# The last batch's Gram products moved behind the third mixing, its softmax and mixing beside twelve early expert units

## The chip, the cores and the metric

The kernel runs on one core of a Trainium2 chip. The metric is the device time of one execution in microseconds (us), lower is better. A core has engines that each work through their own queue in order and wait for one another by semaphores: TensorE (PE, matmuls, with a weight load "PEld" ahead of each), VectorE (DVE), ScalarE (ACT), GpSimd (POOL, here only the issuer of indirect DMAs) and SyncE (SP, the issuer of plain DMAs). A matmul writes to PSUM, and ACT or DVE copies it out from there.

## The reference

Four batches of column-normalised channel attention, followed by a mixture of eight experts with one expert for each token:

```python
B, N, C = (4, 5056, 256)                 # q, k, v; in all 20224 tokens
qn = q / (np.linalg.norm(q, axis=1, keepdims=True) + 1e-06)
kn = k / (np.linalg.norm(k, axis=1, keepdims=True) + 1e-06)
s = kn.transpose(0, 2, 1) @ qn / tau
s = s - s.max(-1, keepdims=True)
a = np.exp(s)
a /= a.sum(-1, keepdims=True) + 1e-09
x = (v @ a)                              # 256 x 256 per batch, then N x 256

logits = x @ w_gate                      # E = 8 experts, hidden width 1024
e_idx = np.argmax(logits, axis=1)
gate_w = softmax(logits)[rows, e_idx]
eom = 1.0 / (1.0 + np.exp(-(x @ w_output_gate)))
h = np.maximum(x[mask] @ w1[e], 0.0)     # for each expert e, its tokens
out[mask] = gate_w[mask, None] * eom[mask, e, None] * (h @ w2[e])
```

## The kernel before

**Attention.** `gram(b)` reads q and k of a batch in 20 steps of 256 rows (tile `qk`, six buffers, loaded by SP). A step squares q and k on ACT (`sq`, L396), adds the squares on DVE (`acc`, L397), and adds eight matmuls (L409) to the 256 x 256 product in `s_ps`. After the 20 steps come twelve stages of the softmax: the copy `s_sb` (L418), the norms `k_ps` (L425), their spread over the columns `n_ps` (L447), the exponential (L458), the transposes `at_ps` (L467), the gate columns `aw_ps` (L477), and the split of the result into a high and a low part, `ah` and `al` (L489, L490). Pauses (`yield`) stand between the stages so that other work can be put beside them.

`mix(b)` needs `ah` and `al` of its batch. It has 20 steps of 256 tokens in five groups of four. A step turns v on PE (`turn`: `vt_ps` L519, cast `vh` L523 on ACT, rest `vl` L525 on DVE), does twelve matmuls into `x_ps` (L549 to L551), and copies them to `st` on ACT (L552). Three stages follow the 20 steps. At the end of a group, `route` finds the expert of each of its 1024 tokens with some fifteen small DVE rows and a few on ACT. Two steps later it counts the tokens of each expert with nine small matmuls (`r_ps`, L611 and L614), works out slots from the running counts `rco` (L619 to L624), and POOL scatters the group's rows to regions by expert in DRAM (`xs_d`, L627), in eight indirect DMAs.

**Experts.** `blocks` works in units of 256 (later some of 128) tokens of one expert: `fetch_x` reads their rows (`xg`; by SP for the units below 20, L894), `prepare` scales and splits them (`b_id` L913, `b_mx` L916, some small DVE rows, `xr` L946 on ACT and L947 on DVE, two transposing DMAs `xt` L951), `h_part` does four parts of twelve matmuls (`h_ps`, L972 to L974, copied out at L976 and L977), `y_part` four parts of twelve (`y_ps`, L996 to L998, copied out to `yo` at L1002), and `store` scatters the result by two indirect DMAs on POOL (L1009). A unit's y parts run beside the next unit's h parts; one `yield` of `blocks` is one such pair of parts, 24 matmuls. `x_ps`, `h_ps` and `r_ps` share four PSUM buffers; `vt_ps` and `y_ps` share three.

**Early units.** The place of a unit's rows depends on the counts. `checkpoint(False)` ranks the experts by their counts so far (`rank_experts`), has POOL read back a word of `xs_d` behind the scatters (`mark`, L640), from which it is known that they have landed, and fills the table of slots `gi` for the first units: L824 for the units of the fullest expert, L753 for the others. Here ten units run from it (`EARLY`), of which seven (`FIRST[1]`) are surely of the fullest expert. `checkpoint(True)` does the same for all others after the last mixing.

**Weights.** `prep_first` and `prep` bring an expert's weights (`raw`, 1 MB for each half), find the scale (L328 on ACT), split them into two 16-bit parts (L349 on ACT, L350 on DVE) and store these to DRAM (`wsc`, L358). `fetch_w` on POOL gathers them for a unit (L865). The fullest expert's weights stay in `wbuf`, and no fetch is needed for its units. `raw` of the later experts uses the four buffers of `st`.

**Order.** The bottom of the kernel writes the order out by hand: `_beside(main, (gen, rate))` takes `rate` steps of `gen` for each step of `main`. Gram 0 runs alone; its softmax beside the first steps of gram 1; mixings 0 to 2 beside the grams that are left, 1.3 steps for each of mixing; then `checkpoint(False)`, and the fourth mixing with no gram beside it, with the fullest expert's weights and from its twelfth step the first units. From this order a planner, which has its own idea of what each instruction costs, makes the queue of every engine: an instruction that is ready in its simulation may go ahead of one that is not. `main(...)` notes an instruction, and `behind` or `in_turn` tie others to places behind it on the same engine.

## Time and profile before

| | us |
|---|---|
| runs | 1291.0 (median of 3), 1288.16 to 1294.69 |
| the profiled execution | 1285.2, its span 1283.4 |
| PE busy in the span | 1201.1 (94%) |
| DVE, ACT, POOL busy | 702.2, 620.3, 572.5 |
| first matmul of a unit | at 374.67 |

The numbers of the profile are of one execution. A row of the windows view gives, for a stretch of the span, its length and then each engine's busy time with its instructions, the share of full speed that TensorE's clock was granted, the mean busy share of the 16 DMA engines, and what they moved. A row of the timeline is start, duration, engine, line, operation, tiles, count and the idle time before it with what ended it. A row of the chain is start, duration and what the end of the program hung on at that time.

### The profile page before, as it was taken

How to read it: one execution, taken by the hardware profiler on the slowest of the kernel's cores; microseconds unless marked ns; L12 is line 12 of the kernel's file. 1: busy time of each engine (PE TensorE's matmuls, PEld its weight loads, DVE VectorE, ACT ScalarE, POOL GpSimd, SP SyncE). 2: the span in 40 equal slices, each digit the busy share in tenths (PEclk: the TensorE clock that was granted, in tenths of full speed). 3: DMA queues.
4: the chain of work that ended last, by engine and by line, in shares of the span. 5: the costliest groups of instructions: out<-in, count | busy, mean ns of one | idle time of the engine just before them, and what ended most of it. 6: DMA issues, size and time to landing. Idle time of an engine off the chain costs nothing.

```text
span 1283.4 us, 27742 instructions
## 1 busy us (share of the span) xinstructions
PE 1201.1 (94%) x10412; PEld 1075.3 (84%) x10412; DVE 702.2 (55%) x2123; ACT 620.3 (48%) x1233; POOL 572.5 (45%) x561
## 2 busy tenths in 40 slices
PE   8999999997766989999999999999999899999998
PEld 7898888896755878888888888888888789999997
DVE  6666647544646765546464566544444454555552
ACT  5666557445633555545364556433333333444442
POOL 0004654555466123445454455544445454444443
PEclk9999999897989999999999999999999999999999
DMA  8976776754547895556555554843333534346743
GB/s 294 333 239 219 251 251 222 241 161 156 184 157 197 219 251 142 143 142 142 142 143 142 142 142 110 234 107 77 68 72 100 161 66 88 78 77 165 202 108 133
DMA packets 174594, 208.54 MB, mean 162 GB/s; under 512 B 120904, under 2 KB 123982, under 8 KB 169464
## 3 DMA queue, kind: packets, MB, share of 16 engines
q1 hardware_dynamic: 130312, 126.84, 35.7%
q0 software_dynamic: 43312, 79.73, 21.4%
q8 instruction: 84, 1.38, 0.4%
q14 instruction: 54, 0.44, 0.1%
q10 hardware_dynamic: 832, 0.16, 0.1%
HBM read 275.55 MB, written 61.41 MB: 263 GB/s over the span
## 4 chain that ended last, share of the span: by engine, by line
PE 75%; issue 8%; DMA 5%; DVE 4%; ACT 3%; POOL 2%; another core or an unknown queue 2%; POOLq 0%; SPq 0%; ACTq 0%; DVEq 0%
PE h_ps L974 9%; PE s_ps L409 9%; PE h_ps L972 9%; PE h_ps L973 9%; PE y_ps L998 9%; PE y_ps L996 9%; PE y_ps L997 9%; PE x_ps L549 3%; PE vt_ps L519 3%; PE x_ps L551 3%; PE x_ps L550 3%; DMA qk<-in_k_dram 2%; POOL out_dram L1009 1%; DMA wbuf<-wsc,wi 1%
## 5 line engine op out<-in xcount | busy, mean ns | idle before, releaser
L977 DVE SCALAR_TENSOR_TENSOR hb<-h_ps,hb 128x512 f16<-128x512 f32 (+1 forms) x360 | 227.1, 634 | 368.5 <-ACT hb L976 282.4
L972 PE MATMUL h_ps<-xt,wbuf 128*128 128x256 f16 (+1 forms) x1440 | 367.7, 263 | 8.5 <-issue 3.9
L974 PE MATMUL h_ps<-xt,wbuf 128*128 128x256 f16 (+1 forms) x1440 | 367.8, 263 | 3.6 <-issue 3.6
L973 PE MATMUL h_ps<-xt,wbuf 128*128 128x256 f16 (+1 forms) x1440 | 367.8, 263 | 3.5 <-issue 3.4
L996 PE MATMUL y_ps<-wbuf,hb 128*128 128x256 f16 x1296 | 354.4, 274 | 4.7 <-issue 3.4
L998 PE MATMUL y_ps<-wbuf,hb 128*128 128x256 f16 x1296 | 354.3, 274 | 3.6 <-issue 2.5
L997 PE MATMUL y_ps<-wbuf,hb 128*128 128x256 f16 x1296 | 354.4, 273 | 1.8 <-issue 1.6
L976 ACT ACTIVATE hb<-h_ps 128x512 f16<-128x512 f32 (+1 forms) x360 | 194.3, 550 | 328.8 <-PE h_ps L974 211.9
L627 POOL DMA_INDIRECT xs_d<-st,r_si x160 | 171.3, 1071 | 227.2 <-DVE r_si L623 91.5
L865 POOL DMA_INDIRECT wbuf<-wsc,wi x166 | 175.4, 1056 | 217.0 <-PE h_ps L974 154.0
L1009 POOL DMA_INDIRECT out_dram<-yo,b_id x162 | 168.9, 1043 | 76.0 <-issue 42.8
L972 PEld LDWEIGHTS <-wbuf 128*128 128x128 f16 x1440 | 141.6, 98 | 23.4 <-issue 5.5
L409 PE MATMUL s_ps<-qk 128*128 128x256 f32 x640 | 152.5, 389 | 8.8 <-DMA qk<-in_k_dram 6.3
L973 PEld LDWEIGHTS <-wbuf 128*128 128x128 f16 x1440 | 141.5, 98 | 21.0 <-issue 7.0
L974 PEld LDWEIGHTS <-wbuf 128*128 128x128 f16 x1440 | 141.6, 98 | 18.3 <-issue 4.6
L996 PEld LDWEIGHTS <-hb 128*128 128x128 f16 x1296 | 127.2, 98 | 21.7 <-issue 6.3
L998 PEld LDWEIGHTS <-hb 128*128 128x128 f16 x1296 | 127.2, 98 | 21.6 <-issue 4.6
L409 PEld LDWEIGHTS s_ps<-qk 128*128 128x128 f32 x640 | 120.8, 195 | 23.9 <-DMA qk<-in_q_dram 6.3
L997 PEld LDWEIGHTS <-hb 128*128 128x128 f16 x1296 | 127.2, 98 | 16.3 <-issue 2.1
L881 POOL DMA_INDIRECT xg<-xs_d,gi x49 | 50.8, 1037 | 178.5 <-DVE xr L947 157.7
L549 PE MATMUL x_ps<-ah,vh 128*128 128x272 f32 x320 | 104.5, 327 | 20.7 <-DVE rco L624 8.2
L397 DVE TENSOR_TENSOR acc<-acc,sq 128x1024 f32<-128x1024 f32 x76 | 92.8, 1222 | 44.9 <-ACT sq L396 29.1
(196 smaller groups left out, 1497.2 us busy)
## 6 DMA issues: line engine op xcount, KB each, us to landing
qk<-in_q_dram SPq DMA_DIRECT2D x76, 256.0 KB
qk<-in_k_dram SPq DMA_DIRECT2D x76, 256.0 KB
v<-in_v_dram SPq DMA_DIRECT2D x32, 512.0 KB
raw<-in_moe_w_dram SPq DMA_DIRECT2D x16, 1024.0 KB
xg<-xs_d SPq DMA_DIRECT2D x30, 272.0 KB
wsc<-whi SPq DMA_DIRECT2D x14, 512.0 KB
wsc<-wlo SPq DMA_DIRECT2D x14, 512.0 KB
v<-in_v_dram SPq DMA_DIRECT2D x8, 480.0 KB
```

The lines of the kernel that those rows point to most:

```text
L409: nc.tensor.matmul(s_ps[:, c, :], kt[:, 1, t, c * P : (c + 1) * P], qt[:, 0, t, :], start=st == 0 and t0 == 0 and t == 0 and c == 0 and n ...
L627: ins = nc.gpsimd.indirect_dma_start(out=xs_d[:, :], out_offset=bass.IndirectOffsetOnAxis(ap=si[:np_, t : t + 1], axis=0), in_=st[:np_, t, ...
L865: nc.gpsimd.indirect_dma_start(out=wbuf[half][:, at_of(u), :], out_offset=None, in_=wsc[half][:end, :], in_offset=bass.IndirectOffsetOnAxi ...
L972: nc.tensor.matmul(hp, w1s[:, 0, c, fs], xh, start=fi == 0 and c == 0, stop=False, **KWM)
L973: nc.tensor.matmul(hp, w1s[:, 0, c, fs], xl, start=False, stop=False, **KWM)
L974: main(PE=nc.tensor.matmul(hp, w1s[:, 1, c, fs], xh, start=False, stop=fin, **KWM))
L976: main(ACT=nc.scalar.activation(hh, h_ps[:, :, :w], AF.Relu))
L977: ins = nc.vector.scalar_tensor_tensor(out=hb[:, 1, 2 * fp : 2 * fp + 2, :w], in0=h_ps[:, :, :w], scalar=0.0, in1=hh, op0=ALU.max, op1=ALU ...
L996: nc.tensor.matmul(y_ps[:, t, :], hb[:, 0, f, tsl], w2s[:, 0, f, :], start=st, stop=False, **KWM)
L997: nc.tensor.matmul(y_ps[:, t, :], hb[:, 0, f, tsl], w2s[:, 1, f, :], start=False, stop=False, **KWM)
L998: main(PE=nc.tensor.matmul(y_ps[:, t, :], hb[:, 1, f, tsl], w2s[:, 0, f, :], start=False, stop=fin, **KWM))
L1009: ins = nc.gpsimd.indirect_dma_start(out=out[:, :], out_offset=bass.IndirectOffsetOnAxis(ap=un["id"][:, t : t + 1], axis=0), in_=un["yo"][ ...
```

## The change

The grams of batches 1 and 2 still run beside mixings 0 and 1 (1.2 steps for each). Of the last batch's gram only a few steps run beside the third mixing (0.25 for each of its steps, one for each of its last three); the others follow it, together with the weights of the fullest expert. The ranks are taken after four of the third mixing's five groups, so `SURE`, the tokens surely counted, falls from 52 to 48 blocks, and `FIRST` from 0, 7, 13, 20, ... to 0, 6, 12, 18, .... `EARLY` is 12 instead of 10: six units of the fullest expert and six whose weights may be another's, so the second expert's weights are prepared during the last mixing too. The last softmax runs beside the first twelve steps of `blocks`, and the whole last mixing beside `blocks` at 0.9. The units from the third on take the tiles `acc`, `s_sb` and `at`, which the softmax has left, for `xt`. The last mixing starts its own v tiles and loads them one ahead. Lines that only rename a variable are cut.

```diff
-    EARLY = 10
+    EARLY = 12
...
-    SURE = -(-((B - 1) * N - E * (BLK - 1)) // BLK)
+    SURE = -(-((B - 2) * N + (NG - 1) * GROUP - E * (BLK - 1)) // BLK)
...
+    VLEAD = 1
     RLATE = 2
-    GRATE = 1.3
-    PRATE = 1
-    ALONE = 18
-    LATE = 12
+    GRATE = 1.2
+    G3RATE = 0.25
+    FRATE = 1
+    MARK = 1
+    SOFT = 1
     MWAIT = 12
-    BRATE = 0.7
+    BRATE = 0.9
...
+        keep = lambda **ins: main(**ins) if alone else None
...
-                    nc.scalar.activation(sq, qp, AF.Square)
-                    nc.vector.tensor_tensor(out=acc, in0=acc, in1=sq, op=ALU.add)
+                    keep(ACT=nc.scalar.activation(sq, qp, AF.Square))
+                    keep(DVE=nc.vector.tensor_tensor(out=acc, in0=acc, in1=sq, op=ALU.add))
...
+                            keep(PE=ins)
...
+    def load_v(n):
+
+        while len(vts) <= n:
...
+            vt = ld.tile([P, 4, C], F32, tag="v", name=f"v{b}_{g}_{h}", bufs=VB)
+            main(SP=nc.sync.dma_start(vt[:np_], vg[:, 4 * h : 4 * h + 4, :]))
+            vts.append(vt)
+
+    def turn(b, j):
+
+        n, i = divmod(b * (NG * R // 2) + j, 2)
+        load_v(min(n + (VLEAD if b == B - 1 else 0), B * NG * R // 4 - 1))
...
-        if b == 0:
+        if b in (0, B - 1):
             for j in range(AHD):
-                turn(0, j)
+                turn(b, j)
+        if b == B - 1:
+            yield
...
-            if n < B * total:
+            if n < B * total and (j + AHD < total or b != B - 2):
...
+    def xt_of(u):
+
+        if u < 2:
+            xt = wk.tile([P, CC, 2 * P], F32, tag="vl", name="xt", bufs=XTB)
+        else:
+            if u == 2:
+                both = one.tile([P, 2, 2, C], F32, tag="acc", name="xt_acc")
+                xts.extend(both[:, i, :, :] for i in range(2))
+            if u == 4:
+                xts.append(one.tile([P, CC, C], F32, tag="s_sb", name="xt_s"))
+            if u == 5:
+                xts.append(one.tile([P, CC, C], F32, tag="at", name="xt_at"))
+            xt = xts[(u - 2) % 4]
...
-    for b in range(B - 1):
+    for b in range(B - 2):
         _beside(mix(b), (ahead, GRATE))
     early = checkpoint(False)
+    due = 0.0
+    for i, _ in enumerate(mix(B - 2)):
+        if i == NG * R // 2 - R // 2 + RLATE:
+            next(early)
+        if i == NG * R // 2:
+            alone.append(True)
+            ahead = in_turn(ahead, "PE")
+        due += 1 if alone else G3RATE
+        while due >= 1:
+            due -= 1
+            next(ahead)
+    preps = prep_first()
+    assert behind_last[0] < nstep - 4, behind_last
+    while behind_last[0] < nstep:
+        next(ahead)
+        for _ in range(FRATE):
+            next(preps, None)
+    for i in range(MARK):
+        next(ahead)
+        for _ in range(FRATE):
+            next(preps, None)
     next(early)
-    preps = prep_first()
-    tail = mix(B - 1)
-    for i in range(ALONE):
-        next(tail)
-        if i == LATE:
-            next(early)
-        if i >= LATE:
-            next(run)
-        for _ in range(PRATE):
-            next(preps, None)
+    soft = ahead
+    left = 0
+    for i, _ in enumerate(run):
+        for _ in range(FRATE):
+            next(preps, None)
+        if i < 2:
+            next(soft)
+        else:
+            for _ in range(SOFT):
+                if next(soft, 0) == 0:
+                    left += 1
+        if left:
+            break
     finish(preps)
-    preps = prep(1, E, "st")
-    _beside((next(tail) for _ in range(2)), (run, BRATE))
     finish(early)
-    _beside(tail, (run, BRATE))
+    preps = prep(1, 2, "st")
+    for _ in range(2):
+        next(preps)
     for keep in held:
         keep()
+    tail = mix(B - 1)
+    _beside(tail, (run, BRATE), (preps, 1.0))
+    finish(preps)
     final = checkpoint(True)
     next(final)
+    preps = prep(2, E, "st")
     _beside((next(run) for _ in range(MWAIT)), (preps, SRATE))
```

More of the change, by code (lines that the diff above doesn't have):

```diff
@@ L370, in tile_colnorm_attention_then_top1_moe @@
     a_of = {}
+    alone = []
     def gram(b):
@@ L380, in gram @@
             for i, src in enumerate((q, k)):
-                main = src[b, :MAIN].rearrange("(p t) c -> p t c", p=P)
+                body = src[b, :MAIN].rearrange("(p t) c -> p t c", p=P)
                 nt = TS - 1 if last else TS
@@ L384, in gram @@
                     nc.vector.memset(qk[REM:, i, TS - 1, :], 0.0)
[L385 removed]
+                nc.sync.dma_start(qk[:, i, :nt, :], body[:, t0 : t0 + nt, :])
                 if last:
@@ L390, in gram @@
                 if st == 0 and t0 == 0:
-                    nc.scalar.activation(acc, qp, AF.Square)
+                    keep(ACT=nc.scalar.activation(acc, qp, AF.Square))
                 else:
@@ L408, in gram @@
                         for n, (kt, qt) in enumerate(terms):
-                            nc.tensor.matmul(
+                            ins = nc.tensor.matmul(
                                 s_ps[:, c, :], kt[:, 1, t, c * P : (c + 1) * P], qt[:, 0, t, :],
@@ L503, in tile_colnorm_attention_then_top1_moe @@
     sts = {}
-    def turn(b, j):
-        g, i = divmod(j, R // 2)
-        np_ = LASTP if g == NG - 1 else P
-        if i % 2 == 0:
+    vts = []
+    def load_v(n):
+        while len(vts) <= n:
+            b, m = divmod(len(vts), NG * R // 4)
+            g, h = divmod(m, R // 4)
+            np_ = LASTP if g == NG - 1 else P
             rows = slice(g * GROUP, g * GROUP + np_ * R)
             vg = v[b, rows].rearrange("(p t) c -> p t c", t=R)
-            vt = ld.tile([P, 4, C], F32, tag="v", name=f"v{b}_{g}_{i}", bufs=VB)
-            main(SP=nc.sync.dma_start(vt[:np_], vg[:, 2 * i : 2 * i + 4, :]))
-            sts["v"] = vt
-        vp = sts["v"][:, 2 * (i % 2) : 2 * (i % 2) + 2, :]
+            vt = ld.tile([P, 4, C], F32, tag="v", name=f"v{b}_{g}_{h}", bufs=VB)
[4 more added lines that the diff above has]
+        load_v(min(n + (VLEAD if b == B - 1 else 0), B * NG * R // 4 - 1))
+        vp = vts[n][:, 2 * i : 2 * i + 2, :]
         t_ps = ps_t.tile([P, CC, 2 * P], F32, tag="t", name="vt_ps")
@@ L900, in tile_colnorm_attention_then_top1_moe @@
     xr_of = []
+    xts = []
+    def xt_of(u):
[10 more added lines that the diff above has]
+            xt = xts[(u - 2) % 4]
+        return xt.bitcast(F16).rearrange("p c (a m) -> p (c a) m", a=2)
     def prepare(u):
@@ L942, in prepare_rows @@
         xr16 = xr_of.pop(0)
-        xt = wk.tile([P, CC, 2 * P], F32, tag="vl", name="xt", bufs=XTB)
-        xt = xt.bitcast(F16).rearrange("p c (a m) -> p (c a) m", a=2)
+        xt = xt_of(u)
         for t in range(nt):
@@ L1059, in tile_colnorm_attention_then_top1_moe @@
     grams = [gram(b) for b in range(B)]
-    for _ in range(NT // TS):
+    nstep = NT // TS
+    for _ in range(nstep):
         next(grams[0])
-    ahead = chain(*grams[1:])
+    ahead = chain(*grams[1 : B - 1])
     for _ in grams[0]:
@@ L1065, in tile_colnorm_attention_then_top1_moe, with count @@
             next(ahead)
+    behind_last = [0]
+    def count(gen):
+        for _ in gen:
+            behind_last[0] += 1
+            yield
+    last_gram = count(grams[B - 1])
+    ahead = chain(ahead, last_gram)
     run = blocks(0, NUNIT - TAIL)
-    for b in range(B - 1):
+    for b in range(B - 2):
         _beside(mix(b), (ahead, GRATE))
     early = checkpoint(False)
-    next(early)
-    preps = prep_first()
-    tail = mix(B - 1)
-    for i in range(ALONE):
-        next(tail)
-        if i == LATE:
-            next(early)
-        if i >= LATE:
-            next(run)
-        for _ in range(PRATE):
-            next(preps, None)
+    due = 0.0
[19 more added lines that the diff above has]
+            next(preps, None)
+    next(early)
+    soft = ahead
+    left = 0
+    for i, _ in enumerate(run):
+        for _ in range(FRATE):
+            next(preps, None)
+        if i < 2:
[6 more added lines that the diff above has]
+            break
     finish(preps)
-    preps = prep(1, E, "st")
-    _beside((next(tail) for _ in range(2)), (run, BRATE))
     finish(early)
-    _beside(tail, (run, BRATE))
+    preps = prep(1, 2, "st")
+    for _ in range(2):
+        next(preps)
     for keep in held:
         keep()
+    tail = mix(B - 1)
+    _beside(tail, (run, BRATE), (preps, 1.0))
+    finish(preps)
     final = checkpoint(True)
     next(final)
+    preps = prep(2, E, "st")
     _beside((next(run) for _ in range(MWAIT)), (preps, SRATE))
```

1 line of the change is left out of this document (removed).

## The prediction

> **What bounds the kernel now.** I read the page's slices first, then the windows view by stages, then the waits and timelines of the one stage that is thin.
>
> ```profile
> PE 1201.1 (94%) x10412; PEld 1075.3 (84%) x10412; DVE 702.2 (55%) x2123; ACT 620.3 (48%) x1233; POOL 572.5 (45%) x561
> ...
> PE   8999999997766989999999999999999899999998
> ...
> PEclk9999999897989999999999999999999999999999
> ```
>
> PE is busy 94% of the span, and the other engines are little over half busy at most. The PE row has one hole: slices 10 to 13 (32 us each), where its clock is lower too. The windows view puts numbers on it.
>
> ```profile
> core 0: us, PE busy (x) PEld busy (x) DVE busy (x) ACT busy (x) POOL busy (x), PEclk, DMA share, GB/s
> 64.00:96.00 32.00, 32.00 (x216) 29.71 (x215) 22.13 (x42) 22.22 (x42) 0.00 (x0) 1.00 0.72 241
> 96.00:288.00 192.00, 180.13 (x1236) 165.61 (x1235) 112.72 (x303) 109.09 (x240) 104.14 (x95) 0.97 0.69 224
> 288.00:320.00 32.00, 22.64 (x158) 21.07 (x157) 15.02 (x58) 16.50 (x43) 16.91 (x18) 0.80 0.46 160
> 320.00:384.00 64.00, 46.36 (x345) 43.84 (x344) 35.98 (x151) 33.97 (x83) 34.74 (x34) 0.86 0.52 171
> 384.00:416.00 32.00, 21.59 (x173) 16.13 (x173) 18.72 (x93) 9.89 (x25) 19.09 (x19) 0.95 0.68 183
> 448.00:480.00 32.00, 27.95 (x243) 24.12 (x242) 19.25 (x49) 19.64 (x33) 9.81 (x9) 0.95 1.03 263
> 512.00:576.00 64.00, 62.81 (x576) 55.81 (x575) 32.93 (x92) 31.66 (x59) 30.91 (x29) 1.00 0.54 142
> ```
>
> I call a stage's length less its PE busy time times the granted clock its loss: what it would save if PE ran through at full clock. That gives 0 for the first softmax beside gram steps (64 to 96), 17 us or 9% for mixing with grams (96 to 288), 13.9 for the last softmax beside the end of the third mixing (288 to 320), 24.1 or 38% for the last mixing, bare of grams (320 to 384), 11.5 for the start of the units (384 to 416), and 1.2 or 2% for units alone (512 to 576). **The hole costs 13.9 + 24.1 + 11.5 = 49.5 us**, and no engine is full in it: work is missing that doesn't depend on what is late. The waits inside the hole name what is late:
>
> ```profile
> PE x_ps L549 <- DVE rco L624: 8.2, 2, 7.6
> PE x_ps L549 <- ACT st L552: 4.8, 3, 3.0
> POOL mark L640 <- DMA xs_d<-st,r_si: 5.0, 1, 5.0
> ```
>
> (Each row: microseconds in all, times, the longest.) PE waits for a group's running counts and for copies out of PSUM, round trips over ACT and DVE that a gram's matmuls would cover. The clock goes with it. Of these two rows of the chain, the first is just behind a PE stop, the second later in the same burst:
>
> ```profile
> 293.22 0.23 PE x_ps L550
> 299.06 0.13 PE x_ps L549
> ```
>
> One matmul takes 0.23 us instead of 0.13 for about 4.8 us behind the stop at 291.9, at which clock a long stop costs some 2 us more.
>
> **The change, part by part.** No unit, matmul, scatter or weight is removed; the matmuls are rearranged. First the durations:
>
> ```profile
> 329.88 0.44 PE vt_ps L519 x4
> 331.82 0.44 PE vt_ps L519 x4
> 91.47 1.73 PE s_ps L409 x8
> ```
>
> A mixing step is 331.82 - 329.88 = 1.94 us of PE, a gram step 1.73. Units give 576 matmuls in 64 us, so a part (24) is 2.67 us and a unit (96) 10.7.
>
> **Taken away: the hole, 49.5 us, and two smaller things.** The third mixing's beginning loses its 9% now too; that loss is replaced. The windows view of L549 alone, the first of a step's three kinds of x_ps matmul, counts it (80 for each mixing; busy time of PE and of its weight loads, clock, DMA):
>
> ```profile
> 224.00:256.00 32.00, 8.02 (x25) 5.00 (x25) 0.89 0.72 242
> 256.00:288.00 32.00, 12.64 (x41) 7.57 (x41) 1.00 0.52 163
> 288.00:304.00 16.00, 6.83 (x20) 4.25 (x19) 0.79 0.49 165
> 304.00:320.00 16.00, 2.64 (x6) 1.62 (x6) 0.81 0.44 154
> ```
>
> Eighty back from 320 begins near 239, so 49 us before 288 lose 9%, 4 us. And 448 to 480 loses 5.4, where ACT waits to reuse the second expert's split weights until they are stored:
>
> ```profile
> 456.24 10.83 DMA wsc<-whi
> ```
>
> That split moves into the last mixing, where the same wait may come back: I credit 2, bounded by -5 and +5. In all 49.5 + 4 + 2 = 55.5 us go.
>
> **Added: the third mixing with few grams.** Counting the driver's steps: twelve gram stages run beside gram 0's softmax, 27 beside each of the first two mixings; the two middle grams take 64 of these 66, so the last gram stands at step 2, takes 5 more in the mixing's 20 steps and 3 in its end stages, and 10 remain. PE has 20 x 1.94 + 8 x 1.73 + some 1.5 for counts = 54 us. At the 9% of mixing with grams it loses 5, at the bare mixing's price 24. There are 8 gram steps where a full share is 20 or more, but no weights are split on ACT meanwhile, as they are in the bare stage now. I take 11, somewhat nearer the first. POOL scatters a group in eight pitches of 0.97 + 0.30:
>
> ```profile
> 361.53 0.97 POOL L627 DMA_INDIRECT xs_d<-st,r_si  x1 [0.30 <-issue]
> ```
>
> 8 x 1.28 = 10.2 us for each group, against 54 / 5 = 10.8 on PE, so POOL keeps up, barely. After step 18 come the scatters of the fourth group (some 2 + 10.2), the wait for their landing (5.0, above) and the read of the mark, about 20 us; PE has until the gram's end 2 x 1.94 + 13 x 1.73 = 26 us. The mark is covered. If POOL first scatters the fifth group, it comes some 4 us after the gram's end.
>
> **Added: the gap between the last gram and the first unit.** Behind the gram's last DVE row stands the table of slots, and then a chain that PE can't begin a unit without:
>
> ```profile
> 353.85 0.23 DVE L824 TENSOR_SCALAR gi<-fj,tb_em 128x7 int32<-128x7 f32 x1
> 358.36 0.31 DVE L913 COPY b_id<-xg 128x2 int32<-128x2 int32 x1 [0.57 <-DMA xg<-xs_d]
> 363.53 0.90 ACT L946 ACTIVATE xr<-xg,b_sx 128x256 f16<-128x256 f32 x2
> 370.15 2.62 SPq L951 DMA_TRANSPOSE xt<-xr  x2
> 374.67 0.44 PE L972 MATMUL h_ps<-xt,wbuf 128*128 128x256 f16 x1
> ```
>
> As it ran it took 374.67 - 353.85 = 20.8 us, of which several were ACT and DVE held up by the mixing. Without that: 4.5 to the rows' arrival, 1.9 of DVE (estimate from its rows), 1.4 for the split, 4.5 for the transposes: 12.3, and about 1 from PE's last gram matmul to `gi`. The softmax's own matmuls fill 2.5 of it, and the clock costs 2 afterwards. I take 13, between 9 and 22. The softmax isn't longer than its cover: the chain has the first one's beginning and last matmul, 25 us apart beside full gram steps.
>
> ```profile
> 45.19 0.57 ACT s_sb L418
> 69.83 0.80 PE aw_ps L477 x8
> ```
>
> In the change it has 13 us of gap and then the seven parts that `blocks` issues in these twelve steps: four with h alone (5.3) and three full ones (8.0), 26 in all.
>
> **Added: the first units against the softmax.** Three `prepare` must follow one another fast, and on DVE each is b_mx, two xr and a handful of small rows:
>
> ```profile
> L916 DVE TENSOR_REDUCE b_mx<-xg 128x2 f32<-128x512 f32 x90 | 56.2, 625 | 0.0
> L947 DVE SCALAR_TENSOR_TENSOR xr<-xg,b_sx,xr 128x256 f16<-128x256 f32 x162 | 71.9, 479 | 3.5 <-ACT xr L946 1.9 <-issue 0.8 <-ACT whi L328 0.7
> ```
>
> 0.63 + 2 x 0.48 + about 1 is 2.6 us; three make 8, with four copies of `hb` (0.63 each) and some 5 us of softmax rows 15.5 us of DVE, against 13.3 of PE. Bounds 0 and 11.5 (what the start loses now); I take 6.
>
> **Added: the last mixing beside units.** 20 x 1.94 + 21 parts x 2.67 = 95 us of PE. Units alone lose 2%, mixing with grams 9%, bare mixing 38%: 2, 8.5 or 58 us. Its mixture is nearest to mixing with grams: 8.5. The v loads, two raw loads and four stores that pass through SP here are issued ahead of need by a planner that lets ready DMAs overtake; if they weren't, one v load behind 4 MB would be a stop of some 10 us, inside the bounds.
>
> The added losses are 11 + 13 + 6 + 8.5 = 38.5, the sum 55.5 - 38.5 = **17 us faster**. The profiled execution has 1285.2, 5.8 below the median of 1291.0; 17 off it is 1268, and off the median, which I forecast, **1274 us**.
>
> [...] Single scatters are longer where DVE splits weights:
>
> ```profile
> 350.60 1.89 POOL L627 DMA_INDIRECT xs_d<-st,r_si  x1 [0.31 <-issue]
> 350.51 1.18 DVE L350 SCALAR_TENSOR_TENSOR wbuf<-raw,wsw,wbuf 128x512 f16<-128x512 f32 x1
> ```
>
> 1.89 us instead of 0.97. [...]
>
> **The rivals.** *It packs well*: the lower bounds hold, 5 + 9 + 0 + 2 = 16 lost, 40 us gained, 1251. For it: the first softmax lost nothing. Against: no such dense stage beside PSUM buffers shared by two kinds of work is in this trace.
>
> *The hole only moves* (the change doesn't do what it says): the third mixing is as bare as the fourth was (24), the gap takes its 20.8 and the clock (22.8), the rest as above: 61 against 55.5, 1296.
>
> *The twelve units run out before the final table.* At the last mixing's end `blocks` has made 33 steps, 28 of them parts: 7 units. Five are left, 53 us, with 7 us of parts since the last mixing matmul 60. Today's last mixing matmul is
>
> ```profile
> 382.27 0.29 PE L551 MATMUL x_ps<-ah,vl 128*128 128x272 f32 x1
> ```
>
> The table's rows, by their count, durations, and first and last start:
>
> ```profile
> L753 DVE TENSOR_SCALAR gi<-tb_sl,tb_pm x5: 220/229/239, 390.5 to 443.4; 128x3 int32<-128x3 f32 x2, 128x18 int32<-128x18 f32 x2, 128x44 int32<-128x44 f32 x1
> ```
>
> Now it is 443.4 - 382.3 = 61 us to the table and, with 20.8, 82 to a matmul. If that doesn't shrink, 22 us are lost: 1296. Against: the order puts the table only twelve parts (32 us) after the mixing's end.
>
> *POOL becomes the bound of the last mixing*: every scatter at 1.89 + 0.3 gives 17.5 us a group, two unit stores 2.4 more, 20 against PE's 17.4 for four steps: 2.6 x 5 = 13 lost, 1287.
>
> *Slower: the last mixing stalls beside units as it did bare.* Place: `x_ps`, `h_ps` and `r_ps` take turns in four PSUM buffers, so one late copy on ACT or one late count on DVE stops mixing and units together, where a gram with a buffer of its own would have gone on. It makes the kernel slower from a loss of 26 us, 21% of that stage, on; at 30%, midway to the bare 38%, it loses 41, 32 more than I took: 1306.
>
> **How the numbers follow.** Forecast 0.42, packing well 0.22, the hole moving 0.08, running out 0.10, POOL 0.04, stalling beside units 0.14. 0.5%, about what a measurement of this kernel can tell from no change, is 6.5 us. Faster (the first two) 0.64; within it (1287 to 1296) 0.22; slower 0.14. The forecast's own range is 1260 to 1286. The range over the cases is 1250 to 1306, whose ends are the packed case and the stalled one; what lies beyond is under 2 in 10.
>
> **What would show it.** Right: gram matmuls until some 20 us behind the third mixing's last one; then one PE gap of 10 to 15 us; 95 us of mixing with h and y matmuls at a loss under 10%. Wrong: a wait of x_ps for `rco` or `st` in the third mixing as large as now; a gap over 20 us before the first h_ps; `h_ps` or `x_ps` waiting for `st` or `hb` in every group of the last mixing; DVE waiting for the mark near the twelfth unit.

## The result and the profile after

The changed kernel takes **1350.99 us** (median of 4 runs, 1347.75 to 1358.38) where the kernel before takes 1289.58 on the same chip: ratio **1.049 [1.042, 1.056]**. Forecast were 1274 us, and a range that ended at 1306. The sign was wrong, by more than any rival had it.

The page of the changed kernel's profiled execution (1350.97 us, span 1349.3; total busy time, then busy tenths in 40 slices of 33.7 us, then the granted clock):

```profile
PE 1231.3 (91%) x10412; PEld 1088.3 (81%) x10412; DVE 707.7 (52%) x2125; ACT 623.0 (46%) x1233; POOL 567.6 (42%) x563
...
PE   8999989778699787979999999999999999999998
...
PEclk9898998788798888989999999999999999999999
```

TensorE does the same 10412 matmuls. The hole, four slices wide before, is now a thin stretch from slice 8 to slice 18, and the clock is below 0.9 in nine of these eleven slices. The windows view gives the stages (columns as before: PE, weight loads, DVE, ACT and POOL busy, clock, DMA share, GB/s): third mixing, rest of the last gram, gap, first units beside the softmax and the last mixing's beginning, the last mixing beside units, its last scatters beside units (no `x_ps` matmul is left in this row), units alone, and two rows in which the next experts' weights are prepared.

```profile
240.00:308.00 68.00, 51.22 (x361) 48.37 (x361) 26.56 (x94) 27.82 (x75) 36.86 (x37) 0.82 0.48 155
308.00:342.00 34.00, 28.00 (x115) 21.82 (x113) 17.69 (x74) 12.96 (x22) 14.05 (x15) 0.85 0.64 222
342.00:357.30 15.30, 2.39 (x11) 1.59 (x12) 12.63 (x38) 9.91 (x12) 6.89 (x6) 0.66 0.60 182
357.30:416.00 58.70, 57.20 (x492) 51.19 (x492) 38.00 (x117) 37.39 (x80) 9.42 (x10) 0.97 0.68 206
416.00:500.00 84.00, 65.59 (x497) 56.20 (x497) 33.84 (x116) 30.29 (x74) 34.88 (x36) 0.86 0.35 108
500.00:544.00 44.00, 36.39 (x248) 26.85 (x247) 26.04 (x109) 16.42 (x29) 24.13 (x23) 0.80 0.63 176
544.00:576.00 32.00, 32.00 (x296) 28.68 (x295) 18.54 (x58) 15.12 (x29) 12.49 (x12) 1.00 0.42 133
576.00:640.00 64.00, 54.86 (x461) 46.68 (x460) 32.46 (x90) 30.00 (x54) 25.18 (x25) 0.92 0.52 136
640.00:704.00 64.00, 60.45 (x547) 52.78 (x545) 30.79 (x89) 29.71 (x55) 29.59 (x28) 1.00 0.54 142
```

In losses (length less PE busy times clock) that is 26.0, 10.2, 13.7, 3.2, 27.6 + 14.9 = 42.5, 0 and 13.5 + 3.5 = 17.0, 112.6 in all. The kernel before does the same matmuls from 240 to 640; it loses 57.8 up to 480 and 2.6 behind that. So the two dear stages are the two mixings with their scatters, not the gap. The waits of TensorE from 240 to 600 (line waiting, what released it, us in all, times, longest):

```profile
PE x_ps L563 <- issue: 12.2, 8, 3.7
PE n_ps L452 <- DVE dq L450: 10.6, 1, 10.6
PE w_ps L336 <- DVE wtot L335: 10.1, 2, 6.9
PE r_ps L628 <- issue: 5.9, 6, 1.9
```

The second row lies in the forecast gap: a matmul of the softmax waits for the softmax's own DVE rows, and the first unit's matmul behind it waits 1.3 us more for its transposed rows (`xt`), which end the gap. The first and the last row are something that no rival spoke of: TensorE stands, and no semaphore that the profile shows holds it ("issue"). Every such stop of over 0.4 us between 240 and 544 lies in the second half of a run of eight or more GpSimd transfers, or just behind it. The trace of before has such stops too, in its hole; there I had read the loss as round trips over ACT and DVE.

Theory A is that a long unbroken run of indirect transfers on GpSimd stalls TensorE by itself. Theory B is my slower rival: mixing and units hold each other up by shared PSUM buffers and copies in order.

### The profile page after: what moved, and what is told of

Same layout as the page of the kernel before. It is cut to its first block, busy times and chain, and to the rows that moved or that the text cites. A ratio compares the mean times of both kernels' runs of the same rounds, so it can differ in the third digit from the quotient of the medians.

```text
span 1349.3 us, 27724 instructions
## 1 busy us (share of the span) xinstructions
PE 1231.3 (91%) x10412; PEld 1088.3 (81%) x10412; DVE 707.7 (52%) x2125; ACT 623.0 (46%) x1233; POOL 567.6 (42%) x563
## 4 chain that ended last, share of the span: by engine, by line
PE 78%; issue 7%; DMA 6%; DVE 4%; ACT 3%; another core or an unknown queue 1%; SPq 1%; POOL 1%; POOLq 0%; ACTq 0%; DVEq 0%
PE h_ps L1003 10%; PE h_ps L1001 10%; PE h_ps L1002 10%; PE y_ps L1025 9%; PE y_ps L1027 9%; PE y_ps L1026 9%; PE s_ps L413 8%; PE x_ps L563 3%; PE x_ps L565 3%; PE x_ps L564 3%; PE vt_ps L531 3%; DMA qk<-in_k_dram 2%; DMA wbuf<-wsc,wi 1%; DMA wsc<-whi 1%
## 5 line engine op out<-in xcount | busy, mean ns | idle before, releaser
L641 POOL DMA_INDIRECT xs_d<-st,r_si x160 | 167.2, 1045 | 243.5 <-DVE r_si L637 96.6
L1002 PE MATMUL h_ps<-xt_acc,wbuf 128*128 128x256 f16 (+1 forms) x704 | 179.7, 263 | 1.9 <-issue 1.7
L1001 PE MATMUL h_ps<-xt_acc,wbuf 128*128 128x256 f16 (+1 forms) x704 | 179.8, 263 | 1.2 <-DMA wbuf<-wsc,wi 0.8
L1003 PE MATMUL h_ps<-xt_acc,wbuf 128*128 128x256 f16 (+1 forms) x704 | 179.8, 263 | 1.1 <-issue 1.0
L413 PE MATMUL s_ps<-qk 128*128 128x256 f32 x640 | 157.1, 397 | 14.6 <-DMA qk<-in_k_dram 6.4
L1001 PEld LDWEIGHTS <-wbuf 128*128 128x128 f16 x1440 | 143.0, 99 | 30.4 <-issue 8.7
L1003 PEld LDWEIGHTS <-wbuf 128*128 128x128 f16 x1440 | 143.0, 99 | 23.0 <-issue 7.7
L1002 PEld LDWEIGHTS <-wbuf 128*128 128x128 f16 x1440 | 143.1, 99 | 20.6 <-issue 5.3
L413 PEld LDWEIGHTS s_ps<-qk 128*128 128x128 f32 x640 | 124.3, 200 | 34.8 <-issue 9.1
L563 PE MATMUL x_ps<-ah,vh 128*128 128x272 f32 x320 | 107.4, 337 | 25.0 <-issue 16.9
```

The lines of the kernel that those rows point to most:

```text
L413: ins = nc.tensor.matmul(s_ps[:, c, :], kt[:, 1, t, c * P : (c + 1) * P], qt[:, 0, t, :], start=st == 0 and t0 == 0 and t == 0 and c == 0 ...
L641: ins = nc.gpsimd.indirect_dma_start(out=xs_d[:, :], out_offset=bass.IndirectOffsetOnAxis(ap=si[:np_, t : t + 1], axis=0), in_=st[:np_, t, ...
L1001: nc.tensor.matmul(hp, w1s[:, 0, c, fs], xh, start=fi == 0 and c == 0, stop=False, **KWM)
L1002: nc.tensor.matmul(hp, w1s[:, 0, c, fs], xl, start=False, stop=False, **KWM)
L1003: main(PE=nc.tensor.matmul(hp, w1s[:, 1, c, fs], xh, start=False, stop=fin, **KWM))
```

## The experiments

Each group of runs shared a chip with runs of the kernel before, and the groups fell on five chips of two kinds. I call the kinds **clear** and **stalling**; medians in us, ratio to before on the same chip with its 95% interval where there is one:

| chip | kind | before | kernels |
|---|---|---|---|
| 13 | clear | 1218.97 | a_hold 1241.06, 1.018 [1.012, 1.024]; a_spaced 1246.99, 1.024 [1.019, 1.030]; b_spaced 1247.87, 1.023 [1.016, 1.030]; e_bursts 1269.32 (one run) |
| 1 | stalling | 1281.42 | c_after 1342.32, 1.051 [1.043, 1.058]; d_bare 1337.06, 1.045 [1.038, 1.052]; c_before 1278.63, f_bursts 1381.98 (one run each) |
| 10 | clear | 1217.89 | g_split 1223.94, 1.004 [1.001, 1.007]; g_both 1228.73, 1.008 [1.005, 1.011]; a_hold2 1237.85, 1.015 [1.009, 1.021]; a_spaced2 1248.76 (one run) |
| 9 | stalling | 1286.87 | c_after2 1337.17, 1.039 [1.029, 1.049]; g_split2 1316.75, 1.024 [1.016, 1.033]; g_both2 1309.17, 1.017 [1.009, 1.025] |
| 6 | clear | 1220.09 | c_after3 1236.93, 1.016 [1.010, 1.022]; h_split3 1225.27, 1.006 [1.003, 1.009]; c_before2 1221.63 (one run) |

**1. Spaced scatters, tied grams, dummy bursts (chip 13).** e_bursts puts dummy scatters into the kernel before, at the matmul steps of nine late units. a_spaced and b_spaced put GpSimd memsets behind every second scatter of the changed kernel and of the kernel before:

```diff
+            if t % 2 == 2 - 1 and t < R - 1:
+                space(2)      # two memsets of 128x448 on GpSimd
```

a_hold ties the last gram's steps to their places among the third mixing's steps, since the planner had pulled all early ones ahead of that mixing and left the rest behind it:

```diff
-        if i == NG * R // 2:
+        if i == 0:
             alone.append(True)
             ahead = in_turn(ahead, "PE")
-        due += 1 if alone else G3RATE
+        due += 1 if i >= NG * R // 2 else G3RATE
```

> The kernel before, with runs of extra transfers put in among the units that run alone, from the 28th unit on every fourth: 4, 6, 8, 12 and 16 scatters of 128 rows by GpSimd, one right behind the other; then 8 scatters with a GpSimd memset behind each; 8 plain writes of the same size by SyncE; 8 memsets alone; 8 scatters again. They write rows that nothing reads; the output is unchanged. Theory A (a long unbroken run of indirect DMAs on GpSimd slows how fast the other engines get their instructions, and TensorE runs dry some 7 us into it): 4 and 6 cost TensorE under 1 us each, 8 cost 3 to 5 us, 12 some 8, 16 some 13, all of it in waits that the profile puts down to nothing (issue); the spaced 8 cost clearly less than the unbroken 8; memsets cost nothing. Theory B (mixing and units hold each other up through shared PSUM buffers and in-order copies; the scatters only stand beside it): no run of transfers costs TensorE more than 1 us here, where there is no mixing.

> The changed kernel, with two GpSimd memsets (about 1 us by A's estimate) behind every second of a group's eight scatters, in all four mixings. Theory A: the loss of the last mixing beside units (42 us from 416 to 544) falls below 20 us, the third mixing's and the gram's rest lose less too, and the time falls from 1351 to some 1310. Theory B: the loss stays within 10 us of 42, and the time is the same or longer, since routing takes longer.

> The kernel before, with the same two memsets behind every second scatter. Theory A: the hole from 288 to 416 (49.5 us lost) loses 15 to 25 us less, and the time falls from 1290 to some 1270. Theory B: no change or slower.

> The changed kernel, with the last gram's steps tied to their places from the third mixing's first step on, so that the planner can't move them ahead of it. Theory: the third mixing is bare because the planner put its five gram steps in front of it; with them in place its loss of 26 us falls to about 15, and the time by some 10 us to 1341. Rival: a gram step in every four mixing steps is too little to cover anything; the loss moves by under 4 us.

All four were put in terms of the first chip, and this chip took 72 us less for the kernel before than the first one's 1291. The dummy scatters of e_bursts depended on nothing, so they were issued from 317 us on, ahead of real work, in a run of 86 transfers on GpSimd that ends at 430. Its windows view in the midst of that run:

```profile
320.00:360.00 40.00, 37.70 (x345) 33.94 (x346) 35.93 (x161) 20.43 (x54) 31.09 (x30) 1.00 0.80 240
```

GpSimd starts 30 instructions in these 40 us, one every 1.33 us, and TensorE loses 2.3 us in 40 at full clock. **On this chip a run of 86 transfers stalls nothing**, and the waits of TensorE in the whole execution have no "issue" among them. The 50 us that e_bursts costs come later, from weights that wait in GpSimd's queue behind the dummies (12.3 and 8.5 us for the two longest waits of h_ps for wbuf). So the stall could not be tested here, nor could the plain writes by SyncE and the memsets that e_bursts has for comparison. The spaced kernels only pay for the memsets and the order that they force: b_spaced is 29 us over before, and a_spaced some 10 over the changed kernel (ratio 1.024 against 1.016 in section 4). a_hold, 1.018, is as the changed kernel there.

**2. The same question on a chip that stalls (chip 1).** c_after and c_before are the two kernels as they are. d_bare takes the units away from the last mixing's side:

```diff
-    _beside(tail, (run, BRATE), (preps, 1.0))
+    _beside(tail, (preps, 1.0))
```

f_bursts mends e_bursts: the dummies read the unit's own output rows, so they can't be issued early.

```diff
 in store(u), kernel before, behind the two output stores:
+        if u in BURSTS:        # {28: 4, 32: 6, 36: 8, 40: 12, 44: 16, 48: 8, 52: 16}
+            burst(BURSTS[u], un["yo"])
```

> The changed kernel as it is, on the chip of these runs. In its first profile 42.5 us of the last mixing beside the units were lost, and 26.0 in the third mixing, much of it in stalls at the end of each run of eight scatters. Theory A (the runs of scatters hold the engines up, as that chip had it): where the kernel before takes about 1290 us this one takes about 1351 again; where the kernel before takes about 1219 us, as in the runs of the spaced kernels, the runs of scatters cost next to nothing, the last mixing beside the units loses 10 to 15 us and the whole ratio is 1.00 to 1.02. Theory B (mixing and units hold each other up by the shared buffers and the copies in order): the ratio is 1.04 to 1.06 on every chip, and the last mixing beside the units loses 35 to 45 us.

> The kernel before as it is, for its profile on the same chip. Where it takes about 1290 us: losses by stage as in its first profile (25 us in 317 to 383, 12.5 in 383 to 416). Where it takes about 1219 us, theory A has those stages lose 60 to 70 us less together over the whole span, and most of the difference lies where runs of scatters lie; theory B has no reason for a difference between chips at all.

> The changed kernel with the last mixing bare: the expert units that ran while the last softmax went on are followed by the whole mixing, and the next units come behind it. The work is the same. Theory B: what mixing and units cost each other goes; the last mixing loses what a bare mixing lost before (its stage from 288 to 416 lost 50 us, of which 24 stood beside no gram), so some 20 to 30 us against 42, and the kernel is 10 to 20 us faster than the changed one on the same chip. Theory A: bare scatters come in the same runs, and a bare mixing is not shorter than its scatters (5 groups of 8 at 1.28 us = 51 us beside 120 matmul groups of 49 us): the kernel is as fast as the changed one or up to 15 us slower.

> The kernel before with dummy scatters behind the output stores of seven units (28: 4, 32: 6, 36: 8, 40: 12, 44: 16, 48: 8, 52: 16), from that unit's own rows into memory nobody reads, so that they cannot be issued earlier; nothing waits for them but the GpSimd instructions behind. Theory A: TensorE, which has nothing to do with them, stands from about 7 us after the begin of a run to its end: nothing at 4, little at 6, 3 to 5 us at 8 with idle put down to issue, 8 and more at 12 and 16; on a chip with the time of before near 1219 nothing at 8 and perhaps something at 16. Theory B: no idle beyond a wait for the weights that GpSimd fetches behind the run (shown as a DMA wait at the unit after).

f_bursts shows theory A's stall by itself, in one execution. Seven runs of dummies cost 1382.0 - 1278.6 = 103 us, though nothing but GpSimd waits for them. Windows view of f_bursts, around the runs of 7, 17, 21 and 22 transfers (dummies with the unit's own fetches and stores), and last units with no dummy:

```profile
716.00:738.00 22.00, 20.29 (x182) 17.42 (x180) 7.14 (x20) 7.79 (x16) 14.00 (x14) 1.00 0.75 200
...
872.00:899.00 27.00, 15.85 (x102) 10.18 (x100) 7.55 (x25) 5.38 (x11) 16.89 (x18) 0.71 0.28 89
929.00:962.00 33.00, 17.82 (x110) 11.01 (x108) 6.32 (x17) 4.30 (x9) 20.66 (x21) 0.68 0.28 88
...
1052.00:1084.00 32.00, 14.97 (x97) 9.08 (x95) 4.36 (x14) 3.33 (x7) 21.74 (x22) 0.69 0.43 132
1160.00:1180.00 20.00, 20.00 (x209) 18.18 (x208) 8.74 (x30) 7.93 (x18) 10.42 (x11) 1.00 0.43 86
```

Losses: 1.7, 15.7, 20.9, 21.7 and 0 us, so about one microsecond for each transfer of a run of 17 or more, and next to nothing for a run of 7. The three other runs, of 12 and 13 transfers, lose 10 to 11 us each. Whether plain writes or memsets in these places would stall as well was not tried on a chip of this kind. The timeline shows the course. First the run's first transfer and its last; then TensorE just before and after the first stop (start, duration, and in brackets the idle time before it with its releaser):

```profile
929.59 1.04 POOL L898 DMA_INDIRECT xg<-xs_d,gi  x1 [3.87 <-DVE xr L964]
...
955.38 0.97 POOL L255 DMA_INDIRECT dump<-yo,didx  x1 [0.30 <-issue]
```

```profile
936.05 0.27 PE L1013 MATMUL y_ps<-wbuf,hb 128*128 128x256 f16 x1
936.89 0.27 PE L1014 MATMUL y_ps<-wbuf,hb 128*128 128x256 f16 x1 [0.57 <-issue]
...
950.36 0.37 PE L1015 MATMUL y_ps<-wbuf,hb 128*128 128x256 f16 x1 [1.69 <-issue]
```

TensorE runs through for 936.05 - 929.59 = 6.5 us of the run, then stops again and again, every few matmuls, to its end. All seven runs of this kernel: 66.9 us idle in their windows, 92.5 lost; the difference is the clock, 0.68 to 0.71 in the three longest, so a stall here costs 92.5 / 66.9 = 1.4 times its idle time. No stop between 929 and 962 is longer than 1.7 us, and the mean clock there is 0.68.

d_bare's last mixing nearly without units (first row: all 240 `x_ps` matmuls, and 30 of units), and the units behind it beside the last scatters (second row: no `x_ps` matmul):

```profile
381.00:450.00 69.00, 52.09 (x377) 47.22 (x376) 33.56 (x110) 37.94 (x90) 25.61 (x26) 0.86 0.67 234
450.00:480.00 30.00, 15.12 (x89) 9.11 (x90) 9.89 (x51) 3.19 (x8) 19.74 (x20) 0.67 0.45 154
```

They lose 24.2 and 19.9, 44.1 in all; c_after, on the same chip, loses 35.0 in its last mixing and the scatters behind (395 to 535). The bare mixing's 24.2 is in B's range of 20 to 30, and 8.7 us of it are a wait for the next expert's weights (`w_ps`). For the second row B has no reason: units stand there with no mixing matmul, beside a run of 20 transfers, and 13.4 us of TensorE's waits end in "issue". The row from 500 to 544 of the first profile, 14.9 lost, is of the same sort. The kernel is 5.3 us faster than c_after, inside both intervals; B wanted 10 to 20, A none or up to 15 slower. So taking mixing and units apart doesn't remove the loss, though the total alone wouldn't decide.

c_after repeats the first result, 1.051, and c_before the first profile's losses: 23.1 us in 317 to 383 and 10.4 in 383 to 416, where they were 25.0 and 12.5. How c_after's kernel does on a clear chip had to wait for chip 6.

**3. Scatters in halves (chips 10 and 9).** g_split issues the eight scatters of a group of the last mixing as two fours, the second tied two mixing steps later by a small copy of its indices:

```diff
+            if b == B - 1 and t == R // 2:
+                yield
+                si2 = sm.tile([P, R], I32, tag="r_si2", name="r_si2", bufs=2)
+                with behind("DVE"):
+                    nc.vector.tensor_copy(si2, si)
+                si = si2
```

g_both is this and a_hold's edit. On chip 10, with a_hold2 and a_spaced2 repeated from above:

> The changed kernel with the last batch's grams tied to their places between the third mixing's steps (every fourth step) instead of all behind it; run once more since the first run fell on a chip where the kernel before takes 1219 us. On a chip where before takes about 1281 us theory A (a run of more than about five scatters stalls TensorE where short or few instructions stand beside it; in the seven dummy runs the idle was about 1.0 us for each scatter beyond 5.5): the third mixing has 5 grams more beside it, still far fewer than the mixings of before, so of its 26 us some 5 to 10 go; the kernel is 5 to 12 us faster than the changed one (1342 where before takes 1281), ratio 1.040 to 1.047. Theory B (mixing and units hold each other up, nothing else): no change, ratio 1.050. On a chip with before near 1219 us it gives 1.018 again.

> The changed kernel with the eight scatters of each group of the last mixing in two halves of four, the second tied behind VectorE's work two mixing steps later (one small copy of the indices a group). Nothing else. Theory A, on a chip where before takes about 1281 us: five runs of 9 to 14 GpSimd transfers beside the units, 17 us of TensorE idle and about as much in lower clock, become runs of 4 to 5; of the 42 us that this stage loses 20 to 30 go, and the ratio falls from 1.050 to 1.028 to 1.035. Theory B: the stage keeps its 42 us, ratio 1.050. On a chip with before near 1219 us theory A gives next to no change against the changed kernel there.

> Both edits: grams tied between the third mixing's steps, scatters of the last mixing in halves. Theory A, on a chip where before takes about 1281 us: the sum of the two, 25 to 42 us under the changed kernel, ratio 1.018 to 1.031. Theory B: 1.050. On a chip with before near 1219 us as the tied one alone, 1.015 to 1.02.

> The changed kernel with two GpSimd memsets behind every second scatter, run once more since its first run fell on a chip where the kernel before takes 1219 us and no run of scatters stalled anything. On a chip where before takes about 1281 us theory A: the stalls at the end of runs of scatters shrink to under half (idle of TensorE in the third and last mixing from about 45 us to under 20) though GpSimd takes longer for a group; 10 to 30 us under the changed kernel if the longer group isn't itself the bound, else no change. Theory B: only the longer group, 0 to 20 us over the changed kernel.

The chip was clear once more. a_hold2 and a_spaced2 repeat their numbers, so their tests on a stalling chip weren't had. g_split comes to 1.004. On chip 9, which stalls, with the changed kernel as control:

> The changed kernel as it is, as the control of this call. On a chip where before takes about 1281 us: ratio 1.05 again. On a chip where before takes about 1218 us theory A (runs of scatters stall TensorE on the other chip alone) has little left but the gap before the first unit, the gram's wait for its input and waits for weights: 1.005 to 1.02. Theory B (mixing and units hold each other up everywhere): 1.04 or more there too.

> Scatters of the last mixing in halves, again. Where before takes about 1281 us theory A: 1.028 to 1.035, with runs of 4 to 5 transfers in the last mixing and next to no idle put down to issue there; theory B 1.05. Where before takes about 1218 us: 1.004 again, and theory A wants it within 0.8% of the changed kernel.

> Grams tied between the third mixing's steps and scatters in halves, again. Where before takes about 1281 us theory A: 1.018 to 1.031, by 5 to 12 us under the halved one alone; theory B 1.05. Where before takes about 1218 us: 1.008 again.

g_split2 is 1337.2 - 1316.8 = **20 us under the changed kernel**, for five small copies; A wanted 20 to 30, B no change. Its last mixing and the last scatters beside units, and the row behind them:

```profile
389.00:476.00 87.00, 80.20 (x681) 71.60 (x681) 46.91 (x151) 47.51 (x110) 34.01 (x34) 0.96 0.65 198
476.00:512.00 36.00, 26.84 (x197) 18.95 (x196) 19.35 (x97) 7.93 (x18) 24.15 (x25) 0.86 0.35 100
512.00:576.00 64.00, 60.32 (x534) 52.40 (x532) 39.35 (x119) 37.80 (x66) 28.28 (x27) 0.97 0.75 215
```

The first two rows lose 10.0 + 12.9 = 22.9. The control's (below, 394 to 530) lose 18.3 + 14.1 = 32.4. So this stage gave back 9.5 us, and A had 20 to 30 from it. The third row loses 5.5, and the control's 530 to 602 loses 19.0: there TensorE's wait for the next expert's weights (`w_ps`) falls from 11.4 to 3.4 us. A did not speak of that, and it happens on a clear chip too (section 4), so the total lies in A's range by luck. TensorE's waits that end in "issue" fall from 43.8 to 38.0 us in the whole execution. What is left of them is partly in the later groups, where second halves run into other transfers, 10 to 14 in a row.

The tied grams give another 7.6 us by the medians (A: 5 to 12), but the runs of the two kernels overlap, and their profiled executions differ by 1.0 us, so this gain is not located.

**4. The changed kernel on a clear chip (chip 6).** h_split3 halves the scatters of the third mixing's first three groups too.

> The changed kernel as it is, as the control of this call. Where before takes about 1281 to 1290 us: ratio 1.04 to 1.05. Where before takes about 1218 us theory A has 1.005 to 1.02, theory B (mixing and units hold each other up everywhere) 1.04 or more.

> The kernel before as it is, for its profile on this chip. Where it takes about 1218 us theory A: the stages 288 to 317, 317 to 383 and 383 to 416, which lost 50 us in its first profile, lose 20 to 35 us less here, and no idle put down to issue stands at the end of its runs of scatters.

> The changed kernel with the scatters in halves in the last mixing and in the first three groups of the third as well. Where before takes about 1281 to 1290 us theory A: 5 to 12 us under the kernel with the last mixing's halves alone (ratio 1.024), so 1.014 to 1.020, the idle at runs of scatters in the third mixing from 19 us to under 12. If the third mixing is held by the time of GpSimd itself (8 scatters at 1.28 us a group against 14 us of mixing) or by the copies in order, halves change nothing: 1.024. Where before takes about 1218 us: no change against the halved one there (1.004), or 3 to 5 us more for the copies.

The control comes to **1.016**, as A had it. h_split3 is as g_split, and its question, whether halves help the third mixing on a stalling chip, stays open. But the control's windows show what the third mixing loses on each kind of chip. First c_after2, stalling, then c_after3, clear, the same code: third mixing, rest of the gram, gap, first units, last mixing and its last scatters (two rows), and what stands behind them (one row, and three).

```profile
244.00:311.00 67.00, 48.67 (x343) 46.52 (x344) 23.39 (x86) 25.22 (x69) 34.12 (x36) 0.80 0.45 147
311.00:351.50 40.50, 28.49 (x116) 22.34 (x115) 19.15 (x82) 13.14 (x21) 22.19 (x20) 0.83 0.56 200
351.50:365.00 13.50, 2.13 (x10) 1.35 (x10) 10.84 (x30) 9.33 (x11) 0.65 (x1) 0.64 0.55 158
...
394.00:490.00 96.00, 83.59 (x671) 72.22 (x670) 46.36 (x149) 46.91 (x108) 33.71 (x34) 0.93 0.59 178
490.00:530.00 40.00, 31.24 (x229) 23.59 (x228) 21.77 (x100) 9.11 (x20) 26.78 (x27) 0.83 0.33 104
530.00:602.00 72.00, 60.28 (x505) 51.47 (x503) 40.04 (x118) 36.99 (x63) 25.39 (x25) 0.88 0.69 185
```

```profile
219.00:257.00 38.00, 38.00 (x341) 37.76 (x342) 23.89 (x93) 26.04 (x69) 29.16 (x30) 1.00 0.75 240
257.00:288.00 31.00, 25.40 (x118) 21.56 (x116) 17.43 (x75) 12.76 (x20) 16.45 (x17) 0.89 0.71 257
288.00:302.50 14.50, 2.27 (x11) 1.52 (x12) 11.80 (x33) 9.34 (x11) 8.60 (x8) 0.64 0.68 206
302.50:330.00 27.50, 27.48 (x232) 24.29 (x232) 17.98 (x58) 16.78 (x37) 2.00 (x2) 0.94 0.47 95
330.00:410.00 80.00, 76.92 (x675) 70.66 (x673) 46.39 (x148) 47.98 (x110) 33.45 (x34) 0.98 0.70 215
410.00:440.00 30.00, 28.08 (x265) 25.03 (x263) 26.91 (x124) 11.37 (x25) 22.98 (x24) 1.00 0.46 130
440.00:452.00 12.00, 3.66 (x32) 2.93 (x31) 3.46 (x7) 5.82 (x9) 4.71 (x5) 0.74 1.01 342
452.00:490.00 38.00, 38.00 (x333) 33.30 (x332) 20.55 (x59) 18.23 (x32) 17.49 (x17) 0.95 0.46 142
490.00:502.00 12.00, 5.46 (x49) 4.50 (x47) 3.73 (x16) 4.66 (x10) 2.08 (x3) 0.79 0.93 275
```

The third mixing, 341 and 343 matmuls, takes **38 us here and 67 there: it loses 0.0 and 28.1**. The last mixing loses 4.6 + 1.9 = 6.5 and 32.4. The gap loses 13.0 and 12.1, the same on both.

One thing here goes against A. h_split3 is 11.7 us under its control on this clear chip, where A had next to no change from halves. The control loses 9.3 + 1.9 + 7.7 = 18.9 in its last three rows; h_split3 loses 1.4 in that place (445 to 500), with a wait of 1.0 for `w_ps` instead of 9.7. It gives part of this back in its last mixing (13.7 for 6.5, with one wait of 9.0 for `wbuf`). So more than half of what halves gain is not the stall but weights that are ready sooner; why they are is open.

And the kernel before on the clear chip (c_before2), from the end of its third mixing to the middle of the early units:

```profile
277.00:308.00 31.00, 30.25 (x268) 29.58 (x266) 26.01 (x119) 24.62 (x67) 23.56 (x24) 1.00 0.79 269
308.00:338.00 30.00, 25.35 (x201) 24.46 (x201) 22.73 (x84) 21.81 (x52) 17.68 (x18) 0.89 0.61 186
338.00:381.00 43.00, 36.78 (x316) 31.11 (x316) 32.57 (x140) 20.90 (x41) 33.25 (x33) 0.92 0.93 263
381.00:440.00 59.00, 56.69 (x507) 49.95 (x505) 37.97 (x108) 33.94 (x62) 15.62 (x16) 0.97 0.86 245
```

It loses 0.8 + 7.4 + 9.2 + 4.0 = **21.4 us**, with a bare last mixing and all. The hole of the first profile, 49.5 us, whose removal the whole forecast lived on, is less than half as deep where runs of scatters stall nothing.

## Why the prediction was wrong

Its working can be closed in losses of the first pair of profiles. From the forecast -17: third mixing 26.0 for 11, +15.0; rest of the gram, for which I had nothing, +10.2; gap 13.7 for 13, +0.7; first units 3.2 for 6, -2.8; last mixing 42.5 for 8.5, +34.0; weights 17.0 where 7.5 + 2.6 - 2 were left, +8.9; the 4 us of the third mixing's beginning, of which its stage of before lost only 0.8, +3.2; the stages up to 240, 30.9 for 24.8, +6.1. That is +58.3, and the span is 65.9 longer; 7.6 us are not in these losses.

**The step that failed first is the one that bounds the kernel.** "No engine is full in it: work is missing that doesn't depend on what is late." Part of the hole was that. The larger part, 28.1 of 49.5 us, is not there on the clear chip, and I put it down to the stall at runs of scatters. I quoted waits for `rco` and `st` (8.2 and 4.8 us) and let them stand for all of it, though they come to 13 of the hole's 49.5. The rows of the same view that end in "issue" come to 18.4 if only those of over 1 us are taken; the first four are:

```profile
PE r_ps L611 <- issue: 3.4, 3, 1.9
PE y_ps L996 <- issue: 3.1, 2, 1.8
PE h_ps L972 <- issue: 2.9, 3, 1.3
PE vt_ps L519 <- issue: 2.8, 2, 2.2
```

The lower clock of the hole (0.80 from 288 to 320, 0.86 from 320 to 384) is loss too. Unit matmuls don't fill a stall of that origin: f_bursts (20.9 us lost from 929 to 962) and the rows without mixing matmuls (14.9 here, 19.9 in d_bare) show it among units alone. It goes with the scatters, and all 160 were still there.

**Last mixing beside units, 8.5, was 42.5.** I took the price of mixing with grams, as the nearest mixture. On stalling chips that price doesn't carry over: beside gram matmuls runs of scatters cost less (two mixings lost 16.4 us in 96 to 240 of before), and with only mixing or units beside them more (42.5 for this one mixing and its scatters, 44.1 in d_bare). Why grams help is not shown. On the clear chip the term is 6.5, so as a count of engine work 8.5 was sound; by the measure of my rivals, a share of the stage's length, it should have been 9.4. My slower rival gave 41 for this stage, near the measured loss, but by a cause that the clear chip doesn't show, where the same buffers are shared, and that can't act in the rows without mixing matmuls.

**Third mixing, 11, was 26.0.** Two errors. I put eight gram steps beside it; the planner issued the ready ones earlier and left the mixing bare, the rest of the gram behind it. And bare of grams it pays for the kind of chip: 28.1 against 0.0 on the clear one. Of the 28.1 only 7.4 are TensorE's own waits for "issue"; the rest are late copies on ACT and DVE (9.4) and other waits, and the lower clock. None of this is there on the clear chip, so I take it for the same stall, but that is not shown by itself. So the change has two mixings without grams where the kernel before has one. On stalling chips that is most of the result, 15.0 + 34.0 of the 58.3. Tying the grams back returned 7.6 us by the medians, with the reservation above (g_both2 against g_split2); on the clear chip it cost 4.8 (g_both against g_split).

**Rest of the gram, 0, was 10.2.** It stands alone, with scatters beside it. In the later profiles a wait of 3 to 5 us for q and k is part of it on either kind of chip (last row of the waits below); the first profile has no such wait.

**The gap, 13, was 13.7**, and 12.1 and 13.0 in the later runs; the first units against the softmax, 6, were 3.2. These chains of rows were read rightly.

**Weights, a credit of 2, cost 17.0 - 7.5 - 2.6 = 6.9 more.** I bounded that at 5. ACT's wait for the split to be stored came back (4.4 us), and TensorE stood at `w_ps` for the next scale (8.1 us from 544 to 704). On the clear chip a wait for wbuf's fetch joins it, and the weights are the largest part left, in c_after3's waits from 219 to 505:

```profile
PE n_ps L452 <- DVE dq L450: 10.6, 1, 10.6
PE w_ps L336 <- DVE wtot L335: 9.7, 2, 6.5
PE h_ps L1001 <- DMA wbuf<-wsc,wi: 5.1, 1, 5.1
PE s_ps L413 <- DMA qk<-in_k_dram: 4.7, 1, 4.7
```

So even without the stall the change loses: 8.4 + 13.0 + 1.7 + 6.5 + 9.3 + 1.9 + 7.7 = 48.5 from the third mixing's end to 502, against 21.4 of hole (and 0.2 in the 50 us behind it). In those two profiles 14 us came back in the units' last stretch (5.5 lost from 720 on, against 19.5), which I can't put down to the change; the spans differ by 10.9 and the medians by 16.8.

"It packs well" and "the hole only moves" fell as sums: both kept the hole's price as the prize. The twelve units did not run out. The POOL rival's 1.89 us for every scatter did not come: the 27 scatters from 416 to 500 took 25.93 us, 0.96 each, and the 8 behind them 1.17 each.

No version beat the kernel before: the best on a clear chip is g_split, 1.004 [1.001, 1.007], and on a stalling one g_both2, 1.017 [1.009, 1.025]. Whether the loss left there goes with quarters instead of halves, and what the weights would give if they were prepared before the units, was not tried.

## What to carry to other kernels

Before pricing a hole, split its idle time by releaser and ask which part would be there with any work beside it: here the waits that no semaphore of the profile explains stood in the second half of GpSimd's runs of eight or more transfers or just behind them, and they came among units alone too where f_bursts put its dummy runs (66.9 us of idle time in the seven windows). On the stalling chip of f_bursts a run of 7 indirect transfers cost 1.7 us and one of 12 some 10; halving runs of eight by a real dependency on later work gained 9.5 us in its stage (g_split2 against c_after2). Filler on the same engine cost 10 to 29 us on the clear chip and was not tried on a stalling one. When an edit gains what a theory forecast, find the gain in its stage, and run the edit where the theory says it should do nothing: here over half of the gain was there too. And read the issued order, not the written one: a planner that lets ready work overtake can strip the stage that it was meant to cover.

## What the hardware showed that I had not expected

**Chips differ by 5% on one kernel**, 1218 to 1220 us on three and 1281 to 1290 on the others, and a change's ratio differs with them (1.016 against 1.039 to 1.051), so ratios are comparable within a chip only. In the profiles the difference is mostly loss: some 53 us in c_before2 and 99 in c_before, whose spans differ by 57. In the eleven profiles of the clear chips no wait of TensorE is put down to "issue"; in the nine of the others such waits come to between 32 and 96 us.

**A run of indirect transfers can stall TensorE from 6.5 us after its begin to its end** (the run of 21 in f_bursts), at 1.28 us a transfer, and a run of 86 on another chip stalls nothing (e_bursts, 2.3 us lost in 40 at clock 1.00, no wait for "issue"). What the engine waits for is open; no run shows that it is its instructions, as theory A had it for e_bursts.
